# Delta rule and soft mixture of experts on one core: the experts' weights become the moving operand, four experts at a time

## The chip, the cores and the metric

The kernel runs on one core of a Trainium2 chip. The metric is the device time of one execution in microseconds (us), lower is better. Everything is float32. All engines are named as the profile names them: PE is TensorE (PEld its weight loads), DVE VectorE, ACT ScalarE, POOL GpSimd, SP the queue that issues nearly all DMAs.

## The reference

Two blocks, one behind the other. The first is the gated delta rule (4 batch rows, 8 heads, 768 tokens, head size 48), token by token; its output, with the heads side by side, is a matrix x of 3072 tokens by 384. The second sends x through 32 slots, four for each of 8 experts.

```python
k_n = k / (np.linalg.norm(k, axis=-1, keepdims=True) + 1e-06)
for t in range(S):
    y[:, :, t] = einsum('bhd,bhde->bhe', q_t, state)
    v_old = einsum('bhde,bhd->bhe', state, k_t)
    state = state + beta_t * einsum('bhd,bhe->bhde', k_t, v_t - v_old)
x = y.transpose(0, 2, 1, 3).reshape(B * S, H * D)       # 3072 x 384
logits = x @ phi                                        # phi 384 x 32
d = softmax over the tokens of logits;  slot_input = d.T @ x
for e in range(8):                                      # w1[e] 384 x 1024, w2[e] 1024 x 384
    slot_out[e] = maximum(slot_input[e] @ w1[e], 0) @ w2[e]
c = softmax over the slots of logits
return c @ slot_out
```

Each expert has four slots, so each of its two products has four rows; w1 and w2 of all experts are 25.2 MB.

## The kernel before, in words

**First part.** The tokens go in 24 chunks of 32, in six groups of four. `chunk` (L298) carries the state from chunk to chunk and is a chain of small matmuls: psR on the state (L310), psW with the chunk's inverted triangle TT (L324), the state's update psS (L340), the outputs psY (L354, L359). What doesn't depend on the state runs ahead and is interleaved with the chain: `norm`, `prep` (L215 transposes, L230 products of keys and queries, in which four heads write four groups of 32 partitions, L233 a mask), `invert` (elimination by columns on VectorE, L264 and L267, with trips through DRAM: ld, lb, td), `near` (L282 loads TT of the next chunk, L291 KX spreads the keys by heads, on POOL). `route` (L381 to L464) takes a finished group through the logits and the running softmax over the tokens, and adds the group's share to the slots' inputs `sacc` (96 partitions, 4, 32 slots); `dsum` holds the softmax's sums and `Call` the weights over the slots, for the output.

The recording layer sets the order of instructions on each engine; an engine runs its own list strictly in order and waits on semaphores. All DMAs named below are on SP's queue: one that waits holds up everything behind it.

**Weights.** `load_w1` (L162) puts w1 of an expert on 96 partitions, in two DMAs of 48 partitions, each with four rows of 4 KB per partition; `load_w2` (L169) puts w2 on 128 partitions, eight rows of 1.5 KB each. w1 of experts 0 and 1 is loaded early, behind the first V loads (L499). The rest goes to the pool `wp2`, which lies where the first part's tiles lay. Its first DMA waits for the last use of all of them; w1 has four buffers there and w2 five.

**Experts** (L532 to L582). `first(e)`: w1 in pieces of 96 x 128 is the stationary operand, and the four slots of the expert, four columns, move: 32 products, 64 MATMULs, since a float32 product is two. The result lies transposed, hidden units on the partitions. `relu` puts it into the expert's own columns of `hx` (other columns zero). `second(e)`: hx (128 x 32) is stationary, w2 moves, 384 columns; all experts add up in `pso`, 32 x 384. `first(e)` and `second(e - 1)` are merged in the source, but on PE they stand one block behind the other, from expert 2 on.

**Output** (L584 to L594). `cT` holds Call transposed, 32 slots on the partitions. 24 tiles of 128 tokens: one product (L588, 32 rows), a copy from PSUM on ACT or DVE in turn, one DMA of 192 KB.

Of the kernel before, what the change touches and what calls it, by code (L numbers as in the profile page):

```python
# [8 lines left out]
F32 = mybir.dt.float32  # L9
AX = mybir.AxisListType  # L10
ALU = mybir.AluOpType
# [5 lines left out]
def kernel(  # L17
# [35 lines left out]
    NFC = F // P  # L53
    assert G == 2 and B == 4 and GC * U == C and Dm == H * D and NSL == C
# [4 lines left out]
    ps = ctx.enter_context(tc.tile_pool(name="ps", bufs=1, space=PSUM))  # L59
    dp = ctx.enter_context(tc.tile_pool(name="dp", bufs=2, space=bass.MemoryType.DRAM))  # L60
    att = ExitStack()
    io = att.enter_context(tc.tile_pool(name="io", bufs=2))
# [40 lines left out]
    # the same by blocks: partition 32 h + 8 c + u of a group of chunks  # L103
# [55 lines left out]
    NW1 = 2  # L159
    w1t, w2t = {}, {}  # L160

    def load_w1(e, pool, bufs):  # L162
        w1t[e] = pool.tile([GD, 4, F], F32, name="w1t", tag="w1t", bufs=bufs)
        for g in range(G):
            nc.sync.dma_start(
                out=w1t[e][g * D:(g + 1) * D],
                in_=moe_w1[e, g * 4 * D:(g + 1) * 4 * D].rearrange("(h d) f -> d h f", h=4))

    def load_w2(e, pool, bufs):  # L169
        w2t[e] = pool.tile([P, NFC, Dm], F32, name="w2t", tag="w2t", bufs=bufs)  # L170
        nc.sync.dma_start(out=w2t[e], in_=moe_w2[e].rearrange("(t p) d -> p t d", p=P))

# [450 lines left out]
```

## Time and profile before

| | us |
|---|---|
| median of three runs | 919.21 (918.97 to 921.51) |
| profiled execution: span | 919.5 |
| PE, PEld, DVE, ACT, POOL busy | 679.9, 565.6, 299.4, 101.3, 192.9 |
| first part and routing, until sacc is complete | 0 to 736.8 |
| experts, until so begins | 736.8 to 887.9 |
| so and the 24 output tiles, to the end | 887.9 to 919.5 |
| mean granted PE clock | 0.701 |

The profiled execution takes 919.54 us, 0.3 above the median of the runs. The shares of busy time are means over parts with different limits; a stage has to be read from its own window. In the timeline each row gives start, length, engine, line, operation, tiles (out<-in) and, in brackets, how long the engine had been idle and what released it. A MATMUL's own length includes its way through the array; what a row of them costs is the distance from start to start. The profile's clock column comes from events of the throttle.

### The profile page before, as it was taken

To read this page: it belongs to the slowest core of one execution; us is meant where nothing else is said; L and a number is where in the kernel's file an instruction comes from. 1 tells how busy PE (TensorE), PEld (TensorE's weight loads), DVE (VectorE), ACT (ScalarE), POOL (GpSimd) and SP (SyncE) were. 2 spreads that over 40 slices of the span, in tenths; PEclk is the share of its full clock that TensorE was granted. 3 is DMA by queue.
4 is the path that set the end of the run, shared out by engine and by line. 5 is a ranking of instruction groups with operands and counts; after the bars stand their busy time and mean duration, and the time that the engine had idled before them with its cause. 6 is when DMAs were issued, how large, how long until landed. Compare 5 with 4: busy or idle time off the path is not lost.

```text
span 919.5 us, 19108 instructions
## 1 busy us (share of the span) xinstructions
PE 679.9 (74%) x8324; PEld 565.6 (62%) x8324; DVE 299.4 (33%) x816; ACT 101.3 (11%) x223; POOL 192.9 (21%) x347
## 2 busy tenths in 40 slices
PE   1706569069990799807998069996499799999998
PEld 1504569058880688706888058885398696765754
DVE  3267112942139421394213942226421100000011
ACT  0303000021120211102111021111000110000001
POOL 7231213131251213412134111351210200000000
PEclk9999999999995555755557555565555567667765
DMA  6240763023310242102321021000100099990013
GB/s 118 37 85 26 133 115 72 1 52 55 75 20 0 58 70 55 20 0 58 69 55 19 0 58 32 25 2 0 35 13 1 1 266 211 237 231 16 1 60 146
DMA packets 148019, 58.12 MB, mean 63 GB/s; under 512 B 131968, under 2 KB 143328, under 8 KB 147936
## 3 DMA queue, kind: packets, MB, share of 16 engines
q1 hardware_dynamic: 141888, 55.87, 27.9%
q10 hardware_dynamic: 5664, 0.94, 0.6%
q8 instruction: 65, 1.06, 0.5%
q0 software_dynamic: 384, 0.10, 0.1%
q14 instruction: 18, 0.15, 0.1%
HBM read 45.86 MB, written 11.01 MB: 62 GB/s over the span
## 4 chain that ended last, share of the span: by engine, by line
PE 64%; DVE 17%; DMA 6%; POOL 4%; SPq 3%; ACT 3%; issue 2%; ACTq 0%; DVEq 0%; POOLq 0%
PE ph L557 9%; PE psW L324 8%; PE psY L359 7%; DVE pr L264 7%; PE pso L568 6%; PE psS L340 6%; DVE tt L267 6%; PE pt L215 5%; PE pt L385 5%; PE pt L458 3%; PE pout L588 3%; PE psR L310 2%; PE pt L230 2%; PE psY L354 2%; PE pt L379 2%; SPq L77 2%
## 5 line engine op out<-in xcount | busy, mean ns | idle before, releaser
L215 PE MATMUL pt<-ident,Ks 128*128 128x128 f32 x96 | 42.1, 438 | 167.9 <-POOL Ks L199 158.7
L291 POOL TENSOR_TENSOR KX<-Ks,hm 128x192 f32<-128x192 f32 x184 | 91.0, 531 | 354.0 <-PE psS L340 264.4
L215 PEld LDWEIGHTS pt<-ident,Ks 128*128 128x128 f32 x96 | 20.8, 216 | 173.9 <-POOL Ks L199 159.6
L324 PE MATMUL psW<-R,TT 128*128 128x48 f32 x384 | 86.6, 396 | 34.4 <-DMA TT<-td 31.2
L324 PEld LDWEIGHTS psW<-R,TT 128*128 128x128 f32 x384 | 81.1, 311 | 39.4 <-DMA TT<-td 19.1
L557 PEld LDWEIGHTS ph<-sacc,w1t 96*128 96x128 f32 x512 | 87.8, 272 | 3.8 <-issue 3.8
L557 PE MATMUL ph<-sacc,w1t 96*128 96x4 f32 x512 | 88.1, 310 | 0.0
L359 PE MATMUL psY<-U,AT 128*128 128x48 f32 x384 | 83.9, 393 | 0.0
L264 DVE TENSOR_TENSOR pr<-tt,lb 128x31 f32<-128x31 f32 (+15 forms) x186 | 76.7, 413 | 16.2 <-POOL lb L252 11.0
L359 PEld LDWEIGHTS psY<-U,AT 128*128 128x128 f32 x384 | 78.2, 306 | 3.4
L267 DVE TENSOR_TENSOR tt<-tt,pr 128x31 f32<-128x31 f32 (+15 forms) x186 | 73.3, 394 | 5.2
L340 PE MATMUL psS<-U,KX 128*48 128x48 f32 x1472 | 69.8, 271 | 0.0
L340 PEld LDWEIGHTS psS<-U,KX 128*48 128x48 f32 x1472 | 60.8, 181 | 6.3 <-issue 1.7
L568 PE MATMUL pso<-w2t,hx 128*32 128x384 f32 x128 | 58.5, 627 | 1.7 <-DVE hx L561 1.7
L329 DVE TENSOR_TENSOR U<-psW,bta 128x192 f32<-128x192 f32 x48 | 17.2, 358 | 113.4 <-PE psW L324 113.4
L345 DVE TENSOR_TENSOR S<-S,psS 112x384 f32<-112x384 f32 x46 | 25.5, 554 | 87.6 <-PE psS L340 87.3
L233 DVE TENSOR_TENSOR AT<-pt,bdm 128x512 f32<-128x512 f32 x48 | 31.9, 688 | 62.1 <-ACT Lc L232 59.0
L385 PE MATMUL pt<-phi,yT 96*128 96x32 f32 x192 | 45.1, 398 | 6.0 <-ACT yT L381 5.1
L230 PE MATMUL pt<-KQ 48*32 48x64 f32 x1536 | 47.5, 310 | 1.9
L385 PEld LDWEIGHTS pt<-phi,yT 96*128 96x128 f32 x192 | 42.0, 323 | 10.5 <-ACT yT L381 9.1
L561 DVE TENSOR_SCALAR hx<-ph 128x32 f32<-128x32 f32 x8 | 1.5, 192 | 141.0 <-PE ph L557 141.0
L354 PE MATMUL psY<-S,KQ 48*32 48x48 f32 x1536 | 46.1, 265 | 0.1
(107 smaller groups left out, 698.9 us busy)
## 6 DMA issues: line engine op xcount, KB each, us to landing
w1t<-in_moe_w_dram SPq DMA_DIRECT2D x16, 768.0 KB
w2t<-in_moe_w_dram SPq DMA_DIRECT2D x8, 1536.0 KB
Ks<-in_k_dram SPq DMA_DIRECT2D x96, 48.0 KB
V<-in_v_dram SPq DMA_DIRECT2D x96, 48.0 KB
out_dram<-ob SPq DMA_DIRECT2D x24, 192.0 KB
Qs<-in_q_dram SPq DMA_DIRECT2D x80, 48.0 KB
ld<-Lc SPq DMA_DIRECT2D x24, 128.0 KB
lb<-ld SPq DMA_DIRECT2D x6, 512.0 KB
```

The source lines that it names most:

```text
L215: nc.tensor.transpose(tp[:, i, a, :], src[:, c, b * G:(b + 1) * G, :].rearrange("p g d -> p (g d)"), ident)
L230: nc.tensor.matmul(pg[rh, b], lhsT=KQ[cc][r, b, 0, rh], rhs=KQ[cc][r, b, :, rh], start=True, stop=True, skip_group_check=True)
L264: nc.vector.tensor_tensor(prv, tt[:, 0:m, j:j + 1].broadcast_to([P, m, w]), lb[:, j, j + 1:C].unsqueeze(1).broadcast_to([P, m, w]), op=ALU ...
L267: nc.vector.tensor_tensor(tt[:, 0:m, j + 1:C], tt[:, 0:m, j + 1:C], prv, op=ALU.subtract)
L291: nc.gpsimd.tensor_tensor(KX[cc][:, g, b], kn[:, b].unsqueeze(1).broadcast_to([P, 4, D]), hm.unsqueeze(2).broadcast_to([P, 4, D]), op=ALU. ...
L324: nc.tensor.matmul(pw[:, i, g, :], lhsT=T[:, (2 * hf + i) * G + g].rearrange("p h t -> p (h t)"), rhs=Rs[hf][:, i, g, :], start=True, stop ...
L340: nc.tensor.matmul(psS[DP * g:DP * g + D, i, h, :], lhsT=kx[:, g, 2 * hf + i, h, :], rhs=Us[hf][:, i, g, :], start=True, stop=True, skip_g ...
L354: nc.tensor.matmul(py[C * h:C * h + C, b, :], lhsT=kq[r, b, 1, C * h:C * h + C], rhs=old[b // 2][r, b % 2, h, :], start=(b == 0), stop=Fal ...
L359: nc.tensor.matmul(py[:, b, :], lhsT=at[:, g, b].rearrange("p h t -> p (h t)"), rhs=Us[b // 2][:, b % 2, g, :], start=False, stop=True, sk ...
L385: nc.tensor.matmul(pl, lhsT=yT[:, h].rearrange("p c t -> p (c t)"), rhs=phi[:, h, :], start=(h == 0), stop=(h == 3))
L557: nc.tensor.matmul(st["ph"][:, t, :], lhsT=w1t[e][:, h, t * P:(t + 1) * P], rhs=sacc[:, h, sl], start=(h == 0), stop=(h == 3))
L568: nc.tensor.matmul(pso, lhsT=hx[:, e, t, :], rhs=w2t[e][:, t, :], start=(e == 0 and t == 0), stop=(e == E - 1 and t == NFC - 1))
```

## The change

1. **Loads.** w1 of an expert goes to 128 partitions in one DMA (partition p holds rows 3p to 3p + 2, 12 KB in one piece), and so does w2 (rows 8p to 8p + 7, 12 KB in one piece). w1t is 12 KB a partition instead of 16. The contraction index of each product is therefore taken in steps: `sT[:, k::NKT]`, `hr[:, 4 * t4 + i::NFC]`.
2. **Pools.** `wp2` and a new PSUM pool `pp` have `reuse_waits="tile"`: a tile waits only for what lay in its own place. By the addresses that the allocator gives, w1t of experts 2 and 3 lie over K, and over Lc, lb and tt; w2t 0 over tt and TT, w2t 1 to 3 over KQ and AT, w1t 4 and 5 over V, K and Q. The first part's PSUM pool is closed with the first part. The order of the loads is new (w2 in fours), w2 has six buffers, `ob` six instead of four.
3. **Slots.** `sacc` is transposed twice so that the slots' inputs lie with 128 rows of the contraction on the partitions: `sl`, three pieces of 128 x 32.
4. **Products, four experts at a time.** `sl` (128 x 32, all slots) is stationary; w1 of four experts moves, 512 columns a time, each expert writing its own 32 partitions of a PSUM tile. Of the 32 rows that an expert gives, four are its own; the mask `msk` takes the others to zero together with the ReLU, half on ACT, half on DVE. The result is not transposed, so eight transposes (128 x 128) turn it into `hT`. Then 32 columns of hT are stationary per expert, and w2 moves, again four experts on four groups of 32 partitions of `pso`, which is now 128 x 384.
5. **Behind them.** A product with `sel4` adds the four groups and writes the sum into all four; `so` lies four times on 128 partitions. `cT` is made by one transpose per group instead of four. An output tile's product uses the 32 rows of its batch row, so four tiles in turn use four row groups; the PSUM tiles take turns over three names with two banks each instead of two names with two.

Nothing changes in the first part but the tile and the DMAs of w1 for experts 0 and 1.

```diff
     def load_w1(e, pool, bufs):
-        w1t[e] = pool.tile([GD, 4, F], F32, name="w1t", tag="w1t", bufs=bufs)
-        for g in range(G):
-            nc.sync.dma_start(
-                out=w1t[e][g * D:(g + 1) * D],
-                in_=moe_w1[e, g * 4 * D:(g + 1) * 4 * D].rearrange("(h d) f -> d h f", h=4))
+        w1t[e] = pool.tile([P, NKT, F], F32, name="w1t", tag="w1t", bufs=bufs)
+        nc.sync.dma_start(out=w1t[e], in_=moe_w1[e].rearrange("(p k) f -> p k f", k=NKT))
     def load_w2(e, pool, bufs):
-        nc.sync.dma_start(out=w2t[e], in_=moe_w2[e].rearrange("(t p) d -> p t d", p=P))
+        nc.sync.dma_start(out=w2t[e], in_=moe_w2[e].rearrange("(p t) d -> p t d", t=NFC))
...
-    wp2 = ctx.enter_context(tc.tile_pool(name="wts2", bufs=1))
+    wp2 = ctx.enter_context(tc.tile_pool(name="wts2", bufs=1, reuse_waits="tile"))
+    pp = ctx.enter_context(tc.tile_pool(name="pp", bufs=1, space=PSUM, reuse_waits="tile"))
     for e in range(E):
         if e >= NW1:
             load_w1(e, wp2, 4)
-        load_w2(e, wp2, 5)
+        if e % 4 == 3:
+            for i in range(e - 3, e + 1):
+                load_w2(i, wp2, 6)
...
+    nc.vector.tensor_reduce(msk, msk4, axis=AX.X, op=ALU.add)
+    sel4 = wp2.tile([P, 4, C], F32, name="sel4")
+    nc.vector.tensor_reduce(sel4.rearrange("p b t -> p (b t)"),
+                            sel.rearrange("p c h t -> p (h t) c"), axis=AX.X, op=ALU.add)
+    ds4 = wp2.tile([P, 4, NSL], F32, name="ds4")
+    nc.vector.tensor_copy(ds4, dsum.unsqueeze(1).broadcast_to([P, 4, NSL]))
+    pd = bank("tr", [P, 1])
+    nc.tensor.matmul(pd, lhsT=ds4.rearrange("p b s -> p (b s)"), rhs=ones, start=True, stop=True)
...
+    for h in range(4):
+        nc.tensor.transpose(pT[:, h].rearrange("p g d -> p (g d)"), sacc[:, h, :],
+                            ident[0:GD, 0:GD])
+    nc.vector.tensor_copy(sT.rearrange("p (g h d) -> p h g d", g=G, h=4), pT)
+    for k in range(NKT):
+        nc.tensor.transpose(pl[:, k, :], sT[:, k::NKT], ident[0:NSL, 0:NSL])
+    nc.vector.tensor_copy(sl, pl)
...
-            for h in range(4):
-                nc.tensor.matmul(st["ph"][:, t, :], lhsT=w1t[e][:, h, t * P:(t + 1) * P],
-                                 rhs=sacc[:, h, sl], start=(h == 0), stop=(h == 3))
+        def product(f):
+            ph = bank("ph", [P, HF])
+            for k in range(NKT):
+                for j in range(4):
+                    nc.tensor.matmul(ph[C * j:C * j + C], lhsT=sl[:, k, :],
+                                     rhs=w1t[4 * q + j][:, k, f * HF:(f + 1) * HF],
+                                     start=(k == 0), stop=(k == NKT - 1), skip_group_check=True)
+            if f:
+                nc.vector.tensor_scalar(hr[:, HF:F], ph, 0.0, msk[:, q:q + 1],
+                                        op0=ALU.max, op1=ALU.mult)
+            else:
+                nc.scalar.activation(hr[:, 0:HF], ph, ACT.Relu, scale=msk[:, q:q + 1])
+        def turn(t4):
+            pt4 = bank("tr", [P, 4, P])
+            for i in range(4):
+                nc.tensor.transpose(pt4[:, i, :], hr[:, 4 * t4 + i::NFC], ident)
+            (nc.vector.tensor_copy if t4 else nc.scalar.copy)(hT[q][:, 4 * t4:4 * t4 + 4, :], pt4)
...
-            nc.tensor.matmul(pso, lhsT=hx[:, e, t, :], rhs=w2t[e][:, t, :],
-                             start=(e == 0 and t == 0), stop=(e == E - 1 and t == NFC - 1))
+    def second(q):
+        for t in range(NFC):
+            for j in range(4):
+                nc.tensor.matmul(pso[C * j:C * j + C], lhsT=hT[q][:, t, C * j:C * j + C],
+                                 rhs=w2t[4 * q + j][:, t, :],
+                                 start=(q == 0 and t == 0), stop=(q == 1 and t == NFC - 1),
+                                 skip_group_check=True)
...
-        for b in range(B):
-            nc.tensor.transpose(pc[:, b, :], Call[:, n, b, :], ident)
+        pc = bank("tr", [P, P])
+        nc.tensor.transpose(pc, Call[:, n].rearrange("p b s -> p (b s)"), ident)
         nc.scalar.activation(cT[:, n], pc, ACT.Copy)
...
+    first(0)
+    second(0)
+    first(1)
+    second(1)
+    nc.vector.tensor_copy(sj, pso)
+    nc.tensor.matmul(ps4, lhsT=sel4.rearrange("p b t -> p (b t)"), rhs=sj, start=True, stop=True)
+    nc.vector.tensor_scalar(so, ps4, rd, None, op0=ALU.mult)
...
-            po = ps.tile([P, Dm], F32, name="pout", tag=("psR", "psY")[i % 2], bufs=2)
-            nc.tensor.matmul(po, lhsT=cT[:, n, b, :], rhs=so, start=True, stop=True)
-            ob = wp2.tile([P, Dm], F32, name="ob", tag="ob", bufs=4)
+            po = bank(("ph", "tr", "po")[i % 3], [P, Dm])
+            nc.tensor.matmul(po, lhsT=cT[C * b:C * b + C, n, :], rhs=so[C * b:C * b + C],
+                             start=True, stop=True)
+            ob = wp2.tile([P, Dm], F32, name="ob", tag="ob", bufs=6)
```

How the instructions now stand, on the two engines that matter. SP, from the last loads of the first part to the outputs, before (TT<-td is the last chunks' inverse, w1t and w2t the weights, ob an output tile):

```order
L282 DMA TT_213<-td 32x8x32 x4
L171 DMA w2t<-in_moe_w_dram 128x8x384 x2
L165 DMA w1t<-in_moe_w_dram 48x4x1024 x2
L171 DMA w2t<-in_moe_w_dram 128x8x384
L165 DMA w1t<-in_moe_w_dram 48x4x1024 x2
L171 DMA w2t<-in_moe_w_dram 128x8x384
```

and after, the same place:

```order
L281 DMA TT_213<-td 32x8x32 x4
L166 DMA w1t<-in_moe_w_dram 128x3072 x2
L170 DMA w2t<-in_moe_w_dram 128x3072 x4
L166 DMA w1t<-in_moe_w_dram 128x3072 x4
L170 DMA w2t<-in_moe_w_dram 128x3072 x4
L651 DMA out_dram<-ob 128x384 x24
```

The 20 expert loads that took turns are 14, in blocks: w1 of experts 2 and 3; w2 of 0 to 3; w1 of 4 to 7; w2 of 4 to 7. The last two w1 have the places of experts 2 and 3, the last two w2 the places of 0 and 1.

PE, from the end of the routing to the first output tiles, before (pt<-db is the last share of sacc; one row of L557 or L568 is a block of products):

```order
L458 MATMUL pt<-db,Y 96x128 x16
L539 MATMUL pt<-ones,dsum 32x1
L577 MATMUL pt<-ident,Call 32x128 x8
L557 MATMUL ph<-sacc,w1t 128x4 x11
L577 MATMUL pt<-ident,Call 32x128 x8
L557 MATMUL ph<-sacc,w1t 128x4 x11
L577 MATMUL pt<-ident,Call 32x128 x8
L557 MATMUL ph<-sacc,w1t 128x4 x42
L568 MATMUL pso<-w2t,hx 32x384 x16
L557 MATMUL ph<-sacc,w1t 128x4 x32
L568 MATMUL pso<-w2t,hx 32x384 x8
L557 MATMUL ph<-sacc,w1t 128x4 x32
```

and after, the start of the experts (ds is ds4):

```order
L457 MATMUL pt<-db,Y 96x128 x16
L564 MATMUL tr<-ones,ds_6832 128x1
L572 MATMUL tr<-ident,sacc 32x96 x4
L578 MATMUL tr<-ident,sT 128x32 x3
L626 MATMUL tr<-ident,Call 128x128 x3
L594 MATMUL ph<-w1t,sl 32x512
L626 MATMUL tr<-ident,Call 128x128 x2
L594 MATMUL ph<-w1t,sl 32x512 x2
L626 MATMUL tr<-ident,Call 128x128
L594 MATMUL ph<-w1t,sl 32x512 x21
```

and the rest up to the outputs:

```order
L607 MATMUL tr<-ident,hr 128x128 x8
L618 MATMUL pso<-w2t,hT 32x384 x32
L594 MATMUL ph<-w1t,sl 32x512 x24
L607 MATMUL tr<-ident,hr 128x128 x8
L618 MATMUL pso<-w2t,hT 32x384 x32
L636 MATMUL ph<-sj,sel_6830 128x384
```

The 256 products on w1 with four moving columns have become 48 with 512; the 64 on w2 stay 64, in two blocks; dsum's product stands ahead of everything that the experts need.

More of the change, by code (lines that the diff above doesn't have):

```diff
@@ L53 @@
     NFC = F // P
+    NKT = Dm // P
     assert G == 2 and B == 4 and GC * U == C and Dm == H * D and NSL == C
@@ L565, in second @@
[L565 to L573 removed]
+    pT = bank("tr", [NSL, 4, G, D])
+    for h in range(4):
+        nc.tensor.transpose(pT[:, h].rearrange("p g d -> p (g d)"), sacc[:, h, :],
+                            ident[0:GD, 0:GD])
@@ L578 @@
         nc.scalar.activation(cT[:, n], pc, ACT.Copy)
-    for e in range(E + 1):
-        drain(merge(*([second(e - 1)] if e else []), *([first(e)] if e < E else [])))
-    so = cpool.tile([NSL, Dm], F32, name="so")
-    nc.vector.tensor_scalar(so, pso, rd, None, op0=ALU.mult)
+    first(0)
+    second(0)
+    first(1)
+    second(1)
+    sj = wp2.tile([P, Dm], F32, name="sj")
+    nc.vector.tensor_copy(sj, pso)
+    ps4 = bank("ph", [P, Dm])
+    nc.tensor.matmul(ps4, lhsT=sel4.rearrange("p b t -> p (b t)"), rhs=sj, start=True, stop=True)
@@ L584 @@
+    so = wp2.tile([P, Dm], F32, name="so")
+    nc.vector.tensor_scalar(so, ps4, rd, None, op0=ALU.mult)
     for n in range(NG):
```

46 lines of the change are left out of this document (25 added, 21 removed).

## The prediction

> **What bounds the kernel now.** I read the groups by line, then the timeline of the last 190 us, the DMA rates by window, and the chain of waits near the other place where expert weights move. One execution, columns of a group: busy us, mean ns; of a timeline: start, length.
>
> ```profile
> core 0: 919.5 us, clock 0.701
> ```
> ```profile
> L557 PE MATMUL ph<-sacc,w1t 96*128 96x4 f32 x512 | 88.1, 310 | 0.0
> L568 PE MATMUL pso<-w2t,hx 128*32 128x384 f32 x128 | 58.5, 627 | 1.7 <-DVE hx L561 1.7
> L588 PE MATMUL pout<-so,cT 32*128 32x384 f32 x48 | 27.4, 759 | 0.7 <-DVE so L582 0.7
> ```
> ```profile
> 736.53 0.28 DVE L464 TENSOR_TENSOR sacc<-sacc,pt 96x128 f32<-96x128 f32 x1 [0.59 <-PE pt L458]
> ...
> 887.87 0.60 DVE L582 TENSOR_SCALAR so<-pso,rd 32x384 f32<-32x384 f32 x1 [8.32 <-PE pso L568]
> ...
> 916.00 0.56 DVE L591 COPY ob<-pout 128x384 f32<-128x384 f32 x1 [2.00 <-PE pout L588]
> ```
>
> The slots are complete at 736.8, the experts end at 887.9, the last output tile is copied at 916.6, the span ends 2.9 later: 151 us of experts, 31 us of output. TensorE fills both: 88.1 and 58.5 us in the first, 27.4 in the second. The next rows (windows: five engines' busy us, granted clock, DMA share, GB/s) show that the weights are all in when a third of the stage is still to come, and that the output leaves DMA at 0.43.
>
> ```profile
> 102.00:121.00 19.00, 7.72 (x188) 7.26 (x184) 3.18 (x8) 0.66 (x2) 3.76 (x8) 1.00 0.99 170
> 576.50:577.00 0.50, 0.50 (x4) 0.49 (x3) 0.00 (x0) 0.00 (x0) 0.50 (x2) 0.50 1.04 426
> 738.00:745.00 7.00, 7.00 (x54) 6.79 (x54) 0.00 (x0) 1.78 (x4) 0.37 (x1) 0.79 1.01 368
> ...
> 833.00:886.00 53.00, 52.15 (x237) 36.83 (x236) 0.57 (x3) 0.00 (x0) 0.00 (x0) 0.68 0.00 1
> 889.00:917.00 28.00, 26.96 (x48) 13.70 (x46) 6.69 (x12) 5.89 (x12) 0.00 (x0) 0.56 0.43 162
> ```
>
> The same rows give two DMA rates. The window at 576 is lb<-ld (4 KB rows on 128 partitions), the one at 738 mostly the first w2 tiles (128 partitions): 370 to 426 GB/s. The window at 102 is the two preloaded w1 tiles, two DMAs of 48 partitions each: 170 GB/s at the same DMA share. 4 KB rows run at 426 in one and 170 in the other, so I put the difference down to 48 partitions. That slow load stands in the chain of waits:
>
> ```profile
> 100.27 0.45 SPq L165
> ...
> 101.74 19.34 DMA w1t<-in_moe_w_dram
> ...
> 121.44 0.45 SPq L77
> ```
> ```profile
> 121.92 1.91 PE L324 MATMUL psW<-R,TT 128*128 128x48 f32 x8 [12.19 <-DMA TT<-td]
> ```
>
> TensorE stands still for 12.2 us because chunk 1's inverse (TT) queues behind w1.
>
> **The change, step by step** (before's clock; the early gain is taken off at the end).
>
> *Preload.* 3.1 MB on 128 partitions at 400 GB/s take 7.9 us instead of 19.3: 11 us, all on the chain, since the SP queue and TensorE both go on from there in the same order. Bounds 0 (another wait takes over) and 11.5.
>
> *When the weights come.* Before, the first expert DMA behind the first part waits for everything there; afterwards each waits for what lay in its own place.
>
> ```profile
> 658.05 22.83 SPq L282 DMA_DIRECT2D TT<-td  x16
> ...
> 736.57 1.03 SPq L171 DMA_DIRECT2D w2t<-in_moe_w_dram  x2
> ```
> ```profile
> 672.17 3.76 POOL L291 TENSOR_TENSOR KX<-Ks,hm 128x192 f32<-128x192 f32 x8 [23.83 <-PE psS L340]
> ...
> 702.70 1.94 PE L324 MATMUL psW<-R,TT 128*128 128x48 f32 x8
> ...
> 707.06 0.53 PE L354 MATMUL psY<-S,KQ 48*32 48x48 f32 x10
> ```
>
> w1 of experts 2 and 3 need the last KX (675.9) and their turn on SP (680.9); w2(0), w2(1) the last TT read (704.6); w2(2), w2(3), w1(4), w1(5) the last psY on KQ (707.6). 3.1 MB, then 9.4 MB at 400 GB/s: in by 690 and 729. All of the first four experts and half of w1 of the others lie there at 736.8. Behind the 4 TT DMAs of the last chunk nothing in the first part loads anything, so this hides completely; were engines slower under it, a few per cent of 50 us would be the price, but hx took as long at 788 under full DMA as at 843 without:
>
> ```profile
> 788.75 0.19 DVE L561 TENSOR_SCALAR hx<-ph 128x32 f32<-128x32 f32 x1 [24.37 <-PE ph L557]
> ...
> 843.14 0.19 DVE L561 TENSOR_SCALAR hx<-ph 128x32 f32<-128x32 f32 x1 [17.98 <-PE ph L557]
> ```
>
> *Start of the experts.* Gone: 24 transposes on 32 columns, the hx memset. New, in a row after 736.8: on VectorE the sel4 reduction (128x512), msk, ds4; dsum's product, which stands first on TensorE; four transposes of sacc, a copy 32x384, three transposes, a copy 128x96, three of the six Call transposes with their copies through two banks.
>
> ```profile
> L405 DVE TENSOR_REDUCE cm<-lg 128x32 f32<-128x128 f32 x6 | 2.2, 364 | 0.0
> L186 DVE TENSOR_REDUCE ssq<-sq 128x32 f32<-128x1536 f32 x6 | 10.5, 1746 | 3.6 <-POOL sq L185 3.6
> L233 DVE TENSOR_TENSOR AT<-pt,bdm 128x512 f32<-128x512 f32 x48 | 31.9, 688 | 62.1 <-ACT Lc L232 59.0
> L448 ACT ACTIVATE dr<-pt 128x512 f32<-128x512 f32 x6 | 3.6, 597 | 13.5 <-PE pt L443 13.5
> ```
> ```profile
> 709.26 1.07 PE L379 MATMUL pt<-ident,Y 128*96 128x128 f32 x4
> ```
>
> Between 0.36 us for 128 columns and 1.75 for 1536 a reduction over 512 is 0.74; with msk and ds4 1.1. dsum's two passes on 128 columns 0.6 (psW above: 1.94/8 = 0.24 for one); transposes 0.8 and 0.7 (1.07 for four on 128 columns); copies 0.6 (so's length) and 0.3; five hand-overs of 0.1; Call 0.6, chosen. 5.2 us, bounds 3.5 and 7; the hand-overs and Call are what I know least. First product at 742.0. In the hole of first(0) below, L233 and L448 stand for the copies of 512 columns.
>
> *The products.* Which speed TensorE has is read from the spacing of matmuls, since the clock column of the windows lags it by some 10 us:
>
> ```profile
> 789.00 7.46 PE L568 MATMUL pso<-w2t,hx 128*32 128x384 f32 x16 [0.28 <-DVE hx L561]
> ...
> 792.20 0.18 PEld L568 LDWEIGHTS pso<-w2t,hx 128*32 128x32 f32 x1 [0.46 <-issue]
> 792.84 0.18 PEld L568 LDWEIGHTS pso<-w2t,hx 128*32 128x32 f32 x1 [0.46 <-issue]
> 793.39 0.11 PEld L568 LDWEIGHTS pso<-w2t,hx 128*32 128x32 f32 x1 [0.37 <-issue]
> 793.72 0.11 PEld L568 LDWEIGHTS pso<-w2t,hx 128*32 128x32 f32 x1 [0.21 <-issue]
> ```
> ```profile
> 420.92 1.89 PE L230 MATMUL pt<-KQ 48*32 48x64 f32 x64
> ```
> ```profile
> 685.26 0.60 PE L310 MATMUL psR<-S,KQ 48*32 48x48 f32 x32
> ```
>
> 384 columns take 0.64 us, and from 793.4 on 0.32: half and full clock, 4.4 us after this stage's start at 789.0. So 512 columns are 0.85 or 0.43, 64 columns 0.107 at half. L230 writes four 32-partition groups in turn, with different moving operands, at 1.89/64 = 0.03 us each (0.025 without the last one's tail): four run at once. L310 adds two row groups and goes at 0.60/32 = 0.019. Nothing here runs four groups on all 128 rows; the bounds are one at a time and four at once, and I take four, from L230. One rule would temper this: the Trainium skill, "TensorE: Matmul & The Clock Gate", Measured speedup vs the span model, has three column tiles of 512 columns at 2.38 times, not 3; four would be 3.2 times by that, an estimate, and the total about 794.
>
> One fp32 product is two MATMULs. first(0): 24 products, 48 MATMULs of 512 columns, four at once: 5.1 us full, 10.2 half. With 4.4 us at half: 4.4 + 0.57 x 5.1 = 7.3, and 0.7 for Call between them: ends 750.0. Then a hole: the second half's ReLU (0.69), four transposes (0.9), a copy (0.60): 2.3. second(0): 32 products, 64 MATMULs of 384, 5.2 full, 10.3 half; I take 6.2: ends 758.5. Before, one expert took 151/8 = 19 us; here four take 16.5.
>
> *What is late next.* The order on SP (in the section on the change) says which loads now wait behind which product: the last two w1t reuse the places of experts 2 and 3, so they wait for the end of first(0), and the last four w2t stand behind them on the queue. On TensorE, where before products on w1 and w2 took turns by expert, each turn needing one new tile, the second block of 32 pso products needs all four last w2t at its fourth product.
>
> ```profile
> 655.42 2.58 DMA td<-tt
> ```
>
> That 0.52 MB transfer took 1.3 us more than its bytes. From 750.0: 9.4 MB at 400 GB/s, 23.6, and 1.5: the last w2t is in at 775.1, w1(7) at 759.4. first(1) and its hole end near 768, so second(1) waits 7 us, has the half clock again: 4.4 + 0.57 x 5.2 = 7.4, ends 782.6. At 340 GB/s it would be 4 later. Then a copy (0.56), the product on sel4 (0.9 with hand-overs), so (0.60): output starts at 785.
>
> *Output.* 24 tiles; four row groups and six banks instead of one and four.
>
> ```profile
> L591 DVE COPY ob<-pout 128x384 f32<-128x384 f32 x12 | 6.7, 558 | 21.4 <-PE pout L588 21.4
> L593 ACT ACTIVATE ob<-pout 128x384 f32<-128x384 f32 x12 | 5.9, 491 | 162.3 <-PE pout L588 162.3
> ```
>
> Two engines copy a tile per 0.3 us, SP issues one per 0.5 (1.03 for two, above), 0.2 MB at 400 GB/s is 0.49. TensorE in one row group needs 2 x 0.64 = 1.28, as before; with four at once 0.32, by L310. I take 0.53 per tile: 0.9 + 0.5 + 23 x 0.53 + 3 = 16.6; bounds 15 and 31 (no overlap). End 801.7.
>
> **Sum.** 801.7 - 11 = 790.7 against the profiled 919.5; that execution lies 0.3 above the median, so 790.
>
> **The rivals.**
> *The groups overlap half as well* (two at once on 128 rows, or output rows one at a time): first(0) 12.5 instead of 7.3, second(1) 12.5 instead of 7.4, in all 801; or output at 1.28 per tile, 18 more: 809. Against: L230, L310; for: both have only 48 rows. Chance 0.18.
> *w1 stays at 170 GB/s:* no early gain (+11), and 7.9 us of w1(6), w1(7) become 18.5 (+10.6): 812. [...] The rows, 170 against 426 GB/s at equal share, speak against. Chance 0.08.
> *The early gain is swallowed* by another wait: 802. The chain goes straight from w1 into SP's next DMAs, which speaks against. Chance 0.10.
> *One group at a time, full clock:* 20.5 us for each of four stages, no wait for DMA: 839. Chance 0.03.
>
> ```profile
> L310 PE MATMUL psR<-S,KQ x192: 277/278/287, 672.0 to 699.8; 48*32 48x48 f32 x192
> ```
>
> *Slower:* one group at a time, array drained at every change of group, clock at half. 224 MATMULs stream 164 us at half; with that alone the end is 742 + 164 + 5 + 2.5 + 16.6 - 11 = 919, break-even. A short MATMUL by itself lasts 0.28 (the row above), 0.2 beyond its 48 columns; 224 x 0.2 = 45, so 964. Any drain above nothing decides. Against: L230's 0.03, and L568, one group of 32 columns, was given the full clock. Chance 0.01.
>
> **Numbers.** The forecast has 0.60: about 790, own range 780 to 799 by the bounds of the start, the rate and the clock. The overlap and early-gain rivals reach 809; I draw the range 779 to 812. A difference of 0.3% (three runs spread over 2.5 us) is what can be told from no change; faster by more 0.98, same 0.01, slower 0.01.
>
> **What would show it.** w1t in the early chain near 8 us and TensorE's wait for TT near 1; w1t and w2t issued from 670 to 698, not 725; ph MATMULs 0.11 to 0.21 apart; a hole of some 7 us before the second pso block, released by w2t; output tiles about 0.5 apart. Wrong if ph MATMULs stand 0.43 or more apart, if the weights' windows show under 250 GB/s, or if the first part keeps its length.

## The result, and the profile after

The changed kernel takes 791.92 us (median of 4 runs, 791.59 to 794.45), the kernel before beside it on the same chip 920.36 (918.97 to 922.07, 4 runs): a ratio of 0.8614 with a 95% interval of 0.8593 to 0.8635. The forecast was 790, in a range of 779 to 812. The profiled execution spans 792.7 us; all readings below are of it unless another run is named.

First the early place, where before TensorE stood still for 12.19 us: the timeline of TensorE, and the windows view (PE, PEld, DVE, ACT, POOL busy, granted clock, DMA share, GB/s).

```profile
112.43 1.92 PE L323 MATMUL psW<-R,TT 128*128 128x48 f32 x8 [2.12 <-DMA TT<-td]
```
```profile
102.00:110.00 8.00, 8.00 (x203) 7.73 (x200) 3.08 (x8) 0.66 (x2) 1.82 (x4) 1.00 0.95 385
...
697.00:720.00 23.00, 17.54 (x93) 14.83 (x85) 3.73 (x19) 3.77 (x9) 0.40 (x1) 0.50 0.96 406
720.00:727.00 7.00, 5.77 (x31) 5.48 (x31) 0.84 (x3) 0.60 (x1) 5.82 (x18) 0.55 0.00 0
727.00:742.00 15.00, 11.69 (x77) 4.91 (x75) 3.30 (x10) 2.69 (x8) 0.39 (x2) 1.00 0.09 20
742.00:765.00 23.00, 15.25 (x126) 5.18 (x126) 2.13 (x3) 1.41 (x3) 0.00 (x0) 0.97 0.94 399
```

The preloaded w1 now moves at 385 GB/s instead of 170, and the same product stands at 112.43 instead of 121.92. The other rows show the weights in two bursts at about 400 GB/s, with nothing moving between 720 and 740. Why nothing moves there is told by SP's queue: the first eight expert loads go out while the last chunk is still at work, the last six begin with w1 of experts 6 and 7, whose places come free only when the first block of products is done, and the four w2 stand behind these in the queue.

```profile
672.42 0.93 SPq L166 DMA_DIRECT2D w1t<-in_moe_w_dram  x2
695.83 3.76 SPq L170 DMA_DIRECT2D w2t<-in_moe_w_dram  x4
699.64 0.98 SPq L166 DMA_DIRECT2D w1t<-in_moe_w_dram  x2
...
739.88 0.81 SPq L166 DMA_DIRECT2D w1t<-in_moe_w_dram  x2
740.74 7.64 SPq L170 DMA_DIRECT2D w2t<-in_moe_w_dram  x4
```

The expert stage, the timeline of VectorE (first and last row) and of TensorE between them, with what ended the wait ahead of a row in brackets:

```profile
727.61 0.28 DVE L463 TENSOR_TENSOR sacc<-sacc,pt 96x128 f32<-96x128 f32 x1 [0.59 <-PE pt L457]
727.81 1.01 DVE L557 TENSOR_REDUCE sel<-sel 128x128 f32<-128x512 f32 x1
...
773.39 0.56 DVE L634 COPY sj<-pso 128x384 f32<-128x384 f32 x1 [14.32 <-PE pso L618]
```
```profile
731.92 1.05 PE L594 MATMUL ph<-w1t,sl 128*32 128x512 f32 x2
...
734.51 5.37 PE L594 MATMUL ph<-w1t,sl 128*32 128x512 f32 x42
...
742.19 5.37 PE L618 MATMUL pso<-w2t,hT 128*32 128x384 f32 x64 [0.22 <-ACT hT L608]
747.38 1.92 PE L594 MATMUL ph<-w1t,sl 128*32 128x512 f32 x12
750.95 5.34 PE L594 MATMUL ph<-w1t,sl 128*32 128x512 f32 x36 [1.65 <-DMA w1t<-in_moe_w_dram]
...
758.58 0.84 PE L618 MATMUL pso<-w2t,hT 128*32 128x384 f32 x4 [0.23 <-ACT hT L608]
761.85 0.83 PE L618 MATMUL pso<-w2t,hT 128*32 128x384 f32 x2 [2.43 <-DMA w2t<-in_moe_w_dram]
765.47 7.89 PE L618 MATMUL pso<-w2t,hT 128*32 128x384 f32 x58 [2.79 <-DMA w2t<-in_moe_w_dram]
```

Four experts' products on w2, 64 MATMULs of 384 columns, take 5.37 us, 0.32 us for four (one step of the full clock for each group of 32 columns, all four at once). The last block waits twice for w2t, until 765.47, and half its products then run at half clock, in steps of 0.64 until 770.6, as the weight loads show:

```profile
769.95 0.20 PEld L618 LDWEIGHTS pso<-w2t,hT 128*32 128x32 f32 x4 [0.44 <-issue]
770.59 0.14 PEld L618 LDWEIGHTS pso<-w2t,hT 128*32 128x32 f32 x4 [0.44 <-issue]
770.94 0.12 PEld L618 LDWEIGHTS pso<-w2t,hT 128*32 128x32 f32 x4 [0.20 <-issue]
```

The experts are done at 773.4 instead of 887.9. Then the output: the SP queue, and the DMA view of 777 to 792 (packets, MB, share of 16 engines), which says what bounds it:

```profile
777.09 12.77 SPq L651 DMA_DIRECT2D out_dram<-ob  x24
```
```profile
q1 hardware_dynamic: 3456, 4.72, 88.4%
```

24 issues in 12.8 us, 0.53 per tile, with the DMA engines 88% busy where they were at 0.43 before.

### The profile page after: what moved, and what is told of

Its sections match the earlier page's. It is cut to its first block, busy times and chain, and to the rows that moved or that the text cites. A ratio compares the mean times of both kernels' runs of the same rounds, so it can differ in the third digit from the quotient of the medians.

```text
span 792.7 us, 18261 instructions
## 1 busy us (share of the span) xinstructions
PE 549.6 (69%) x7915; PEld 464.8 (59%) x7915; DVE 303.2 (38%) x818; ACT 101.9 (13%) x227; POOL 191.6 (24%) x349
## 4 chain that ended last, share of the span: by engine, by line
PE 58%; DVE 21%; DMA 8%; POOL 4%; ACT 3%; SPq 2%; issue 2%; ACTq 0%; DVEq 0%; POOLq 0%
PE psW L323 10%; PE psY L358 10%; DVE pr L263 8%; PE psS L339 8%; DVE tt L266 7%; PE pt L214 5%; PE pt L384 5%; PE pt L457 4%; PE psR L309 3%; PE psY L353 3%; PE pt L229 3%; PE pt L378 3%; DMA w2t<-in_moe_w_dram 2%; POOL Ks L198 2%; PE pso L618 2%
## 5 line engine op out<-in xcount | busy, mean ns | idle before, releaser
L323 PE MATMUL psW<-R,TT 128*128 128x48 f32 x384 | 86.6, 396 | 24.8 <-DMA TT<-td 21.7
L361 ACT ACTIVATE Y<-psY 128x192 f32<-128x192 f32 x48 | 15.9, 332 | 242.9 <-PE psY L358 242.9
L229 PEld LDWEIGHTS pt<-KQ 48*32 48x32 f32 x1536 | 34.5, 155 | 14.8 <-ACT KQ L217 11.7
L452 POOL TENSOR_TENSOR db<-dr,hm 128x128 f32<-128x128 f32 x96 | 36.1, 414 | 21.4 <-ACT dr L447 20.3
L457 PE MATMUL pt<-db,Y 128*96 128x128 f32 x192 | 37.6, 377 | 4.7 <-POOL db L452 4.5
```

The lines of the kernel that those rows point to most:

```text
L229: nc.tensor.matmul(pg[rh, b], lhsT=KQ[cc][r, b, 0, rh], rhs=KQ[cc][r, b, :, rh], start=True, stop=True, skip_group_check=True)
L323: nc.tensor.matmul(pw[:, i, g, :], lhsT=T[:, (2 * hf + i) * G + g].rearrange("p h t -> p (h t)"), rhs=Rs[hf][:, i, g, :], start=True, stop ...
L452: nc.gpsimd.tensor_tensor(db[:, b], st["dr"][:, c, b].unsqueeze(1).broadcast_to([P, 4, NSL]), hm.unsqueeze(2).broadcast_to([P, 4, NSL]), o ...
L457: nc.tensor.matmul(pa.rearrange("p h s -> p (h s)"), lhsT=Yn[:, c, b, :], rhs=db[:, b].rearrange("p h s -> p (h s)"), start=(b == 0), stop ...
```

## The experiments

Times are of one run unless an interval is given, beside a run of the kernel before on the same chip (918.96 to 921.46). Spans are some 1.7 us shorter than times.

**Row length or width of the loads.** All loads stay on 128 partitions, but in rows of 4 KB (w1) and 1.5 KB (w2) instead of 12 KB.

```diff
-  in_=moe_w1[e].rearrange("(p k) f -> p k f", k=NKT))
+  in_=moe_w1[e].rearrange("(k p) f -> p k f", p=P))
-  in_=moe_w2[e].rearrange("(p t) d -> p t d", t=NFC))
+  in_=moe_w2[e].rearrange("(t p) d -> p t d", p=P))
```

> The changed kernel, but each weight tile is loaded in the rows it had before (w1 4 KB, w2 1.5 KB per row) onto 128 partitions; the contraction index goes in natural order. Theory (the number of partitions sets the rate of a w1 load): w1 and w2 still run at 370 to 420 GB/s, the wait for TT near 112 us stays at 2 us, total 790 to 795. Rival (the length of the rows sets it, 12 KB in one piece against 4 KB): w1 falls back to about 170 GB/s, TT is waited for 12 us again, the last weights come 10 us later, total near 812.

Measured 795.77. Its windows and timeline at the early place:

```profile
102.00:110.00 8.00, 8.00 (x197) 7.73 (x199) 3.08 (x8) 0.66 (x2) 1.58 (x4) 1.00 0.97 360
```
```profile
113.09 1.91 PE L323 MATMUL psW<-R,TT 128*128 128x48 f32 x8 [2.55 <-DMA TT<-td]
```

360 GB/s against 385, the product 0.7 us later. The long rows are worth 1 to 4 us in all (1.4 between the profiled spans, 3.9 from the changed kernel's median); the rest of the gain is not theirs. One thing works for this run: in natural order the first four transposes need only the first half of hr, so the hole behind first(0) is 1.5 us instead of 2.3.

**Width undone.** w1 again on two times 48 partitions in rows of 4 KB, sacc itself stationary in four steps, everything else as in the changed kernel (five w2 buffers, for space).

```diff
+  w1t[e] = pool.tile([GD, 4, F], F32, name="w1t", tag="w1t", bufs=bufs)
+  for g in range(G):
+      nc.sync.dma_start(out=w1t[e][g * D:(g + 1) * D], in_=...)
-  nc.tensor.matmul(ph[C * j:C * j + C], lhsT=sl[:, k, :],
+  nc.tensor.matmul(ph[C * j:C * j + C], lhsT=sacc[:, k, :],
```

> The changed kernel, but w1 is loaded as before (two DMAs of 48 partitions, four rows of 4 KB each), sacc itself is the stationary operand with four steps of 96 rows instead of three of 128, and the transposes of sacc fall away; w2 has five buffers. Theory (48 partitions): w1 at 170 GB/s, so 10 us lost near 112 us and another 10 at the last weights, while products and prologue about cancel (one step in three more on w1, 1.8 us of prologue less): total 808 to 816. Rival (the width doesn't matter, the early gain came from elsewhere): 790 to 796.

Measured 808.75. Its timeline and windows:

```profile
121.61 1.91 PE L326 MATMUL psW<-R,TT 128*128 128x48 f32 x8 [12.09 <-DMA TT<-td]
```
```profile
102.00:110.00 8.00, 7.52 (x190) 7.11 (x186) 3.17 (x8) 0.66 (x2) 2.36 (x6) 1.00 1.01 189
110.00:120.00 10.00, 0.00 (x0) 0.00 (x0) 0.00 (x0) 0.00 (x0) 1.40 (x4) 0.63 1.03 175
...
742.00:765.00 23.00, 16.84 (x132) 5.58 (x124) 1.44 (x2) 1.27 (x2) 0.00 (x0) 0.91 0.91 168
```

The early wait is back in full, and w1 of the later experts is slow as well (168 GB/s). With the run before: rows of 4 KB on 128 partitions go at 360, on 48 at 175 to 189, at the same DMA share of 1.0. The forecast's inference, that 48 partitions were the cause, holds. The run also has two DMAs of 768 KB in place of one of 1536; lb<-ld, with 512 KB on 128 partitions at 426 GB/s before the change, speaks against their size as the cause. The Trainium skill, "DMA: Bandwidth & Descriptors", Rules for kernel authors, says that two transfers to halves of the partitions both use all 16 engines, and advises one transfer to 128 partitions instead; the share near 1 agrees with the first and the rates with the second.

**The early issue alone, undone.** The pool of the expert weights waits again for everything before it.

```diff
-  wp2 = ctx.enter_context(tc.tile_pool(name="wts2", bufs=1, reuse_waits="tile"))
+  wp2 = ctx.enter_context(tc.tile_pool(name="wts2", bufs=1))
```

> The changed kernel, but the pool of the weights waits for all that lay in its region, as before, instead of tile by tile. Theory (after the change the weights' transfer is the bound of the expert stage): all 22 MB behind the preloaded ones start near 728 us and take 55 us, second(1) ends near 792 instead of 773, total near 811. Rival (the products are still the bound and the early loads only fill time): total within 4 us of 792.

Measured 809.91. The first expert load goes out at 725.97:

```profile
725.97 0.83 SPq L166 DMA_DIRECT2D w1t<-in_moe_w_dram  x2
```

The first w2t follows at 726.9 instead of 695.8; 31 us of head start are worth 18 us: behind the change, the transfers set the pace of the experts.

**The early issue alone, done to the kernel before.**

```diff
-  wp2 = ctx.enter_context(tc.tile_pool(name="wts2", bufs=1))
+  wp2 = ctx.enter_context(tc.tile_pool(name="wts2", bufs=1, reuse_waits="tile"))
```

> The kernel before with one thing of the change alone: the second weight pool waits tile by tile, so its loads are issued ahead of the routing. Theory (the kernel before was bound by the tensor engine in its expert stage, and its loads were mostly hidden): 917 to 921. Rival (the early issue carries a good part of the gain by itself): under 914.

Measured 922.64, the kernel before 921.28 (918.98 to 922.33). Its SP queue shows that the loads go out from 681 instead of 737, and nothing comes of it:

```profile
681.34 23.92 SPq L171 DMA_DIRECT2D w2t<-in_moe_w_dram  x2
707.81 0.82 SPq L165 DMA_DIRECT2D w1t<-in_moe_w_dram  x2
```

So the same edit is worth nothing before and 18 us after: what bounded the experts before was TensorE.

**The wide w1 alone, done to the kernel before.** w1 on 128 partitions, slots transposed twice, w1 still stationary: three steps instead of four, 384 MATMULs of four columns instead of 512.

```diff
-  for h in range(4):
-      nc.tensor.matmul(st["ph"][:, t, :], lhsT=w1t[e][:, h, ...], rhs=sacc[:, h, sl], ...)
+  for h in range(3):
+      nc.tensor.matmul(st["ph"][:, t, :], lhsT=w1t[e][:, h, ...], rhs=slt[:, h, sl], ...)
```

> The kernel before with the change's w1 loads and slots alone: w1 on 128 partitions in one DMA, sacc transposed into three pieces of 128 rows; w1 stays the stationary operand, expert by expert, 192 products on w1 instead of 256. Theory (before, TensorE is the bound of the expert stage): 10 us from the early wait for TT, a quarter of the 88 us on w1, about 2 us lost on transposes: total 886 to 894. Rival (DMA was the bound there): the weights are in 30 us earlier, total under 875.

Measured 888.30. Its groups and timeline:

```profile
L565 PE MATMUL ph<-slt,w1t 128*128 128x4 f32 x384 | 63.3, 301 | 0.0
```
```profile
112.74 1.91 PE L321 MATMUL psW<-R,TT 128*128 128x48 f32 x8 [1.95 <-DMA TT<-td]
```

9.5 us from the first part (its sacc is complete at 727.0 + 0.3 instead of 736.5 + 0.3) and 24.8 from a quarter fewer MATMULs on TensorE (63.3 against 88.1), together 34; the span is 32.9 shorter. Of the change's 127 us, the layout of w1 done alone is a quarter; the other three quarters come with the rest of the change together: moving weights in four groups, the early issue and the output.

**One group at a time.** The loop over the experts outside, that over the contraction inside, for both products.

```diff
-  for k in range(NKT):
-      for j in range(4):
+  for j in range(4):
+      for k in range(NKT):
...
-  for t in range(NFC):
-      for j in range(4):
+  for j in range(4):
+      for t in range(NFC):
```

> The changed kernel, but each expert's products stand one behind the other (loop over experts outside, over the contraction inside, in both stages), so that neighbours in the row write the same 32 partitions. Theory (four groups of 32 columns run at once): MATMULs of 512 columns 0.43 us apart instead of 0.11, of 384 columns 0.32 instead of 0.08; four stages of 20.5 us, no wait for the last weights; total 832 to 842. Rival (the gain is the moving operand and the wide loads, not the overlap of groups): total within 10 us of 792.

Measured 815.60, between the two: an order that alternates is worth 24 us, not 40 to 50.

```profile
777.46 17.05 PE L618 MATMUL pso<-w2t,hT 128*32 128x384 f32 x64 [0.23 <-ACT hT L608]
```

17 us for 64 MATMULs, 0.26 from start to start, as in the first such block: less than 0.32 for one at a time. So runs of one expert (16 MATMULs) overlap in part. This block starts so late that it waits for no load, so the 24 us are what is left once the changed kernel's wait of 7 us has gone. Two runs asked how much, with the products on w2 in runs of four and of eight MATMULs, all else as in the changed kernel:

```diff
-  for t in range(NFC):
-      for j in range(4):
+  for j, t in [(j, t0 + t) for t0 in range(0, NFC, R) for j in range(4) for t in range(R)]:
```

With R = 2:

> The changed kernel with one thing undone in part: the products on the second weights stay two products (four MATMULs) long with one expert before they go to the next, instead of one; the products on the first weights as in the changed kernel. From the run with experts one after the other, a reading: a run of 16 MATMULs of 384 columns took 0.26 us each, 4.2 in all, where 16 by themselves at full clock are 5.1; so a change of column group hides some 0.9 us, about three MATMULs, whatever the length of the run. Theory (TensorE has about three MATMULs beyond the running one in hand, and those on another group run at once): a run of four costs 4 x 0.32 - 0.96 = 0.32, 16 runs 5.1 us as one product at a time, in all 790 to 794. Rival (a change of group hides a share of the run, about 0.2 of it): 0.26 each, 16.8 us a stage instead of 5.4, and with the second stage's end at 783.5 in all 801 to 805.

With R = 4:

> As the run before, with four products (eight MATMULs) with one expert before the next. Theory (about three MATMULs in hand): a run of eight costs 8 x 0.32 - 0.96 = 1.6 us, eight runs 12.8 and a tail of 1, so 0.20 to 0.21 each; the first such stage ends at 755 to 756, the second starts with the last weights near 763 to 765 and ends at 777 to 779 instead of 773.4: 796 to 798 in all. Rival (a fixed share is hidden): 0.26 each, 801 to 805. If runs of any length above one overlap alike: 792.

Measured 791.63 and 792.94. The first such stage takes 5.44 us in runs of four and 12.0 in runs of eight (to 752.40; its last three MATMULs stand in rows of their own):

```profile
741.55 5.44 PE L617 MATMUL pso<-w2t,hT 128*32 128x384 f32 x64 [0.23 <-ACT hT L608]
```
```profile
740.39 11.04 PE L617 MATMUL pso<-w2t,hT 128*32 128x384 f32 x61 [0.23 <-ACT hT L608]
```

The weight loads of the run with eight show the pattern (start, length; each step of 0.32 us starts one MATMUL per group that is free):

```profile
742.70 0.11 PEld L617 LDWEIGHTS pso<-w2t,hT 128*32 128x32 f32 x1 [0.21 <-issue]
743.02 0.14 PEld L617 LDWEIGHTS pso<-w2t,hT 128*32 128x32 f32 x3 [0.21 <-issue]
743.34 0.14 PEld L617 LDWEIGHTS pso<-w2t,hT 128*32 128x32 f32 x2 [0.18 <-issue]
743.67 0.14 PEld L617 LDWEIGHTS pso<-w2t,hT 128*32 128x32 f32 x2 [0.18 <-issue]
744.02 0.11 PEld L617 LDWEIGHTS pso<-w2t,hT 128*32 128x32 f32 x1 [0.21 <-issue]
```

Eight MATMULs in four steps, 1.32 us a run: four of the next run lie beside the last four of this one. With 16 the same view repeats every 3.9 us, twelve steps. So a change of group hides four MATMULs in both, not the three that I read from the average; alternating every four or finer gives all of the overlap. That later MATMULs start ahead of earlier ones is seen where this block ends. In the kernel's order of instructions all of second(0) (L617) stands ahead of first(1) (L594), yet three MATMULs of first(1) start at 750.95, before the last three of second(0) at 751.26, 751.59 and 751.91:

```profile
750.95 0.64 PE L594 MATMUL ph<-w1t,sl 128*32 128x512 f32 x3
751.26 0.49 PE L617 MATMUL pso<-w2t,hT 128*32 128x384 f32 x1
```

The stage in runs of eight, forecast at 12.8 and a tail of 1, took 12.0, and most of what it is longer disappeared: its second block starts at 759.84 with weights that are still landing, ends at 771.9, and the total is close to that of the changed kernel, not 796 to 798. A stage twice as long costs nothing here against the changed kernel, whose block stood waiting for the loads and then ran half of its products at half clock. Against runs of four, which kept the full clock, it costs 2.5 us (the block ends 45.8 us behind sacc instead of 43.3).

**Output on one row group.** All output products use the rows of batch row 0, so they can't run side by side (this leaves out the weights over the slots of the other three batch rows).

```diff
-  nc.tensor.matmul(po, lhsT=cT[C * b:C * b + C, n, :], rhs=so[C * b:C * b + C],
+  nc.tensor.matmul(po, lhsT=cT[0:C, n, :], rhs=so[0:C],
```

> The changed kernel, but every output product reads rows 0 to 31 of cT and so, so that all tiles use the same row group of the array; this leaves out the other three batch rows' weights over the slots (each tile gets those of the first). Banks, copies, buffers and DMAs stay. Theory (four row groups run at once): 0.64 us a tile at full clock, 1.28 once the clock is half, the output stage takes 26 to 31 us instead of 17, total 801 to 806. Rival (the six banks and six output buffers made the gain): total within 2 us of 792.

Measured 811.37, worse than either expected. Tiles come every 1.28 us:

```profile
784.19 1.48 PE L644 MATMUL tr<-so,cT 32*128 32x384 f32 x2
785.47 1.48 PE L644 MATMUL po<-so,cT 32*128 32x384 f32 x2
```

Two MATMULs at 0.64: half clock, from 779 to the end, although TensorE is never idle there (from 785 to 795 it is busy 10.00 us of 10.00, at a granted clock of 0.50); 801 to 806 would have needed the full clock for a part of it. In the changed kernel the output falls to the half clock too, at about 780.7 (its MATMULs last 0.84 to 1.00 from there), but four at a time hide it behind the transfers. So the row groups are worth 33 - 17 = 16 us of output.

**The order of the loads.** Two second weights ahead of the two first weights that have to wait for a place.

```diff
-  for e in range(E):
-      if e >= NW1: load_w1(e, wp2, 4)
-      if e % 4 == 3:
-          for i in range(e - 3, e + 1): load_w2(i, wp2, 6)
+  for ld, es in ((load_w1, (2, 3)), (load_w2, (0, 1, 2, 3)), (load_w1, (4, 5)),
+                 (load_w2, (4, 5)), (load_w1, (6, 7)), (load_w2, (6, 7))):
+      for e in es: ld(e, wp2, 4 if ld is load_w1 else 6)
```

> The changed kernel, but w2 of experts 4 and 5, whose places are free, is loaded ahead of w1 of experts 6 and 7, which wait for first(0). Theory (second(1) waits for the last weights, 9.4 MB that start only when first(0) ends): 3.1 MB of them now come in the 12 us before, the last w2 lands 8 us earlier and second(1) keeps the full clock: total 780 to 785. Rival (the wait hides something else that is just as late): total within 2 us of 792.

Measured 785.44 (785.11 to 786.94, 4 runs), 0.8537 of before (0.8505 to 0.8568), just above the 780 to 785 expected. Two more loads go out ahead of the gap, so the transfers run on to about 725 instead of 720 and stand still only from there to 739.5, and the last block hardly waits:

```profile
739.52 0.80 SPq L166 DMA_DIRECT2D w1t<-in_moe_w_dram  x2
747.21 0.80 SPq L170 DMA_DIRECT2D w2t<-in_moe_w_dram  x2
```
```profile
758.26 5.78 PE pso L616 x64
```

The first two rows are of the queue, the third of the chain: the last w2t are asked for when the second block ends, the last block starts at 758.26, waits 0.3 us for them and runs at the full clock.

**Twelve places instead of ten, and the small work moved.** Loads into 12 buffers, the mask and the summed select matrix ahead of the last chunk, the transposes of Call behind the second block on w1 (hr, hT and ob with fewer buffers, for space).

```diff
+  for e in range(NW1, 7): w1_tile(e, wp2, 5)
+  for e in range(7): w2_tile(e, wp2, 7)
+  for ld, es in ((load_w1, (2, 3)), (load_w2, (0, 2, 3)), (load_w1, (4, 5, 6)),
+                 (load_w2, (4, 5, 6, 1))): ...
```

> The changed kernel with twelve buffers for weights instead of ten (hr and hT one buffer, ob four), so that only w1 of expert 7 and w2 of expert 7 wait for a product, loaded in the order of need, and with sel4, msk and ds4 made earlier and Call's transposes moved behind first(1). Theory: prologue 3 us shorter, no wait for w1, the wait before second(1) gone: second(1) ends near 757 instead of 773, total 774 to 779. Rival (the output's four buffers or the products' own chain take it back): 783 to 792.

Measured 809.38 (808.98 to 809.67): a miss by 30 us. Its SP queue:

```profile
672.70 23.73 SPq L186 DMA_DIRECT2D w1t<-in_moe_w_dram  x2
699.02 29.68 SPq L189 DMA_DIRECT2D w2t<-in_moe_w_dram  x3
```

The second of those three w2t loads has a place that overlaps Y, which the routing reads (L476) until the slots are complete at 728; the waits of the queue name that line (us in total, times, longest):

```profile
SPq L189 <- PE pt L476: 28.5, 1, 28.5
```

The queue takes its entries in order, so the eight behind it stood there too, and the kernel was back at the time of the run without early issue. The places had been given by the allocator from the order in which the tiles are made; the expectation had left them out. With six places for w2 none of the early loads lies over Y:

```diff
-  for e in range(7): w2_tile(e, wp2, 7)
-  ... (load_w2, (0, 2, 3)), (load_w1, (4, 5, 6)), (load_w2, (4, 5, 6, 1))
+  for e in range(6): w2_tile(e, wp2, 6)
+  ... (load_w2, (0, 1, 2, 3)), (load_w1, (4, 5, 6)), (load_w2, (4, 5))
```

> The order of the run that loads four second weights ahead of the last two first weights (785.4 us), with a fifth buffer for first weights, so that only one of them waits for the end of the first group's first products; the mask, the summed select matrix and the wide copy of the denominators are made ahead of the last chunk's chain, and the transposes of the combine weights stand behind the second group's first products instead of among the first ones. All tiles that are loaded early lie clear of Y, whose last reader held SyncE's queue in the run before. Theory (what is left is the wait for the last weights and the 3 us of small work among the first products): first products end at 738 to 738.5 instead of 739.5, the last two second weights are asked for at 745 to 746 and land at 754 to 755, the last products start there at the full clock and end at 760 to 761, 19.4 us ahead of the end: 779 to 781. Rival (the tensor engine runs at half clock as long after the quiet stretch whenever it starts, so an earlier start only adds half-clock work): within 1.5 us of 785. If the queue is blocked again, over 800.

Measured 781.75 (779.88 to 785.22, 4 runs), 0.8482 of before (0.8461 to 0.8503): just above the 779 to 781 expected, the fastest version here, and the queue runs free:

```profile
739.00 0.33 SPq L186 DMA_DIRECT2D w1t<-in_moe_w_dram  x1
746.68 0.80 SPq L189 DMA_DIRECT2D w2t<-in_moe_w_dram  x2
```
```profile
759.27 4.72 PE L624 MATMUL pso<-w2t,hT 128*32 128x384 f32 x54
```

The gain over the order alone is 3.7 us by the medians, and less sure than either gain over before: the two intervals nearly meet, and this kernel's runs spread over 5 us. In the profiled execution, the slowest of its four, sacc was complete only at 729.6. Its last block began at 754.43, as expected, but got going only at 759.27: the six transposes of Call, which were to stand ahead of it, stand among its first five products (754.17 to 758.90), and one wait of 0.7 us for w2t falls there too. The span is 783.5, that of the order alone 783.4, so the traces show no gain over it.

## Why the prediction came out right, point by point

| step (us) | forecast | measured |
| --- | --- | --- |
| early gain, to the end of sacc | 11 | 8.9 |
| end of sacc to first product | 5.2 | 4.0 |
| first(0), Call between | 8.0 | 8.0 |
| hole | 2.3 | 2.3 |
| second(0) | 6.2 | 5.4 |
| end of first(0) to last w2t | 25.1 | 25.6 |
| second(1) | 7.4 | 7.9 |
| to the first output product | 2.4 | 2.3 |
| output to the end | 16.6 | 17.1 |

Without second(0) and the hole, which lie beside the loads, the differences make +2.1 - 1.2 + 0.5 + 0.5 - 0.1 + 0.5 = 2.3. The terms add up to 790.5 (roundings on the way made 790.7 of it), and the span is 792.7. The step from 790.7 to 790 took the 919.5 of before for a time, but it is a span: by the 1.7 us between the two, 790.7 is a time of 792.4, beside 794.45 for the profiled execution and 791.92 for the median. That the total is so close is partly luck: an early gain 2.1 too high was set against a start 1.2 too long, and one step came out for another reason than forecast (the clock, below).

*The mechanism* is the forecast's in its main steps: the wide load at the early place, the loads ahead of the routing, four groups at once, then the last six loads behind first(0), which became the bound. The runs bear out each of these by itself: width not row length (795.8 against 808.8), early issue (809.9 without), four groups (815.6 without), row groups of the output (811.4 without), and the new bound (785.4 as soon as the loads are reordered).

*The early gain* was mis-sized. The wait for TT did not go down to 1 but to 2.12 us, since the inverse still queues behind a w1 that takes 8 us. The size of the error is hardly 2 us, however: over the seven profiled executions with the same first part, sacc is complete between 725.8 and 727.6 (plus 0.3), so, against the one profiled execution of before, the gain lies between 8.9 and 10.8, and the profile of the changed kernel is the one at the low end.

*The start* was forecast 1.2 us too long. The reduction on sel took 1.01 instead of 0.74, but it begins before sacc is complete, and VectorE was done with its three operations 1.1 us after that, as forecast. The product on dsum and the seven transposes took 1.5 us with their hand-overs; 2.1 and the hand-overs had been put in.

*The clock.* I took 4.4 us of half clock behind each wait. In first(0) there was none: the windows row of 727 to 742 above has a granted clock of 1.00, and each of the 48 MATMULs lasts 0.59 to 0.62 us. The 2.2 us put in for it went to the transposes of Call, which stand between the first products: 731.92 to 734.51, 2.6 us where 0.7 had been put in. That this step came out at 8.0 is luck. In the run with twelve places, where Call stands elsewhere, the same 48 MATMULs took 5.40 us:

```profile
730.44 5.40 PE L600 MATMUL ph<-w1t,sl 128*32 128x512 f32 x48 [0.35 <-DVE sl L586]
```

Other executions do show the half clock there: in the fastest version first(0) had 0.50 until 735.3, 3.4 us. In the block behind the wait for w2t it was 5.1 us (765.47 to 770.6), and in the run with runs of four none at all behind a wait of the same length: it went from 765.16 in 5.35 us (3.0 us of products lay scattered in that wait, 1.7 in the changed kernel's). The Trainium skill, "TensorE: Matmul & The Clock Gate", Part 1, gives some 3.4 us of work until the full clock and says that the stretch differs from run to run; 3.4 and 5.1 fit that loosely, the blocks without any do not follow from it. What decides stays open here. The prediction also took the clock column to lag by some 10 us. It doesn't: in the kernel before, it reads 0.51 from 789.0 to 793.4 and 1.00 from 793.4 to 796, where the spacing changes too.

*The overlap*: 64 MATMULs of 384 columns in 5.37 us are 0.08 each, where one by itself is 0.32: a full four times. The figure that I cited from the Trainium skill ("TensorE: Matmul & The Clock Gate", Measured speedup vs the span model), 2.38 times for three groups and so, as an estimate, 3.2 for four, was too low for this stream.

*Rivals.* "One group at a time" was priced at 839 and a serial order gave 815.6: the price of an order that doesn't alternate was wrong, as TensorE takes four MATMULs of the next group ahead. "Output one row group at a time" was priced 18 higher; the run gave 19.5 (17.0 between the profiled spans). Against the other three, w1 moved at 385 GB/s, 8.9 us of the early gain came through, and four groups ran at once.

## What to carry to other kernels

When a change makes the engine three times as fast in a stage, ask which load now ends last, and put the loads that wait for a place behind those that don't: one reordering gave 6.5 us of the 7 us wait. An early issue is worth nothing while the engine is the bound and 18 us once the transfers are; price it only against the stage as it will be. One queue takes its entries in order, so before moving loads to the front, look at what lies in each one's place and who reads it last: a single wrong place cost 28 us.

## What the runs showed of the hardware

A load on 48 partitions moved at 168 to 189 GB/s, on 128 at 360 to 406, both at a DMA share of 0.91 to 1.03: the share doesn't tell the rate. Products on different groups of 32 columns ran four at once over all 128 rows, with four different moving operands, and with up to four MATMULs of the next group beside the last ones of this one (4 steps of 0.32 us for a run of eight, 12 for a run of 16); MATMULs of a later block started ahead of the last three of an earlier one. Products on one row group of 32 rows were granted a clock of 0.50 although TensorE was busy without a gap (10.00 us of 10.00, from 785 to 795).
